# Batched cluster-routed attention and a sigmoid-gated FFN on one core: one-pass logits for late pieces, one query group turned by DMA, spare matmuls and half-step places

## The chip, the cores and the metric

The kernel runs on one core of a Trainium2 chip. The metric is device time in microseconds (us) for one execution, a median of runs. The engines are TensorE (PE; its weight loads are shown apart as PEld), VectorE (DVE), ScalarE (ACT), GpSimd (POOL) and SyncE (SP), which here only issues DMAs. Each engine works off its own instructions in the order in which they were written, and waits on semaphores for the others.

## The reference

Inputs are q, k and v of 4 batches x 8 heads x 768 rows x 64 columns, 16 centroids for each head, and three FFN matrices. Each query row and each key row is given to the centroid of its head with the largest dot product; a query attends only to the keys of its own cluster. The output of attention is the input of a gated FFN.

```python
q_assign = np.argmax(np.einsum('bhsd,hcd->bhsc', q_n, c_n), axis=-1)
k_assign = np.argmax(np.einsum('bhsd,hcd->bhsc', k_n, c_n), axis=-1)
mask = q_assign[:, :, :, None] == k_assign[:, :, None, :]
scores = scale * np.matmul(q, k.transpose(0, 1, 3, 2))
scores = np.where(mask, scores, -1000000000.0)
...
gate = 1.0 / (1.0 + np.exp(-(x @ w_gate)))
val = x @ w_val
return (gate * val @ w_out).astype(np.float32)
```

x has 3072 rows and 512 columns, the FFN is 1536 wide. All inputs are float32; the kernel multiplies in float16.

## The kernel before

**Operands.** For each head a tile T holds 12 blocks of 128 columns: blocks 0 to 5 are the keys, 6 to 11 the queries, transposed, so that rows 0 to 63 are the high half of each value in float16. At first rows 64 to 127 hold the low half (the rest of the value), which makes the logits exact enough; after the clusters are picked, rows 64 to 79 are overwritten by a one-hot row of the cluster (keys) or by -1920 times the cluster's complement (queries). One score matmul then gives the masked scores.

**Pieces.** The way of one head from rows to T goes in pieces, whose names stand in the table SCHED: hi (cast to float16; 0 for keys, 1 for queries), lo (subtraction for the low half), tu (transposes on TensorE into PSUM), ev (evacuation to T), lg (logits: T against the centroids), pk (maximum and comparison), ot (the one-hot rows transposed), pl (placed into rows 64 to 79 of T). h1 to h7 are heads 1 to 7 of batch 0, with all keys and the first three query blocks; r0 to r3 are the last three query blocks of pairs 0 to 3 of batch 0, both heads of a pair together; g0 and g1 are heads 0 and 1 of batch 1. The other heads of batches 1 to 3 (names b1p1..., b2...) are transposed by DMA (tn), their one-hot rows too, and copied into T by small DMAs (hp). Pieces of batch 0 and g0, g1 have logits in two passes (`logits2`, L320: for each block one matmul with the high half of the centroids and one with the low half, 16 columns each, added up in PSUM). The others have them in one pass (`logits`, L332: one matmul of 32 columns for each block, a copy of the low half by ScalarE or VectorE, L341, and an addition by VectorE, L349). `b{b}p{p}l2{e}` chooses two passes for one head, if true; `b{b}p{p}le{e}` puts the copy on VectorE, if true.

**Steps.** The attention is a list of steps; a step is one key block against three query blocks of one head: a score matmul (`sc`, L541), an exponential on ScalarE (`es`, L546) and, three steps later (two after batch 0), three matmuls with the values (`av`, L558). Batch 0 has 96 steps: all heads with the first three query blocks (steps 0 to 47), then all with the last three (48 to 95). Each later batch has 96 as well. After the score matmul of a step come, in this order, gate and value matmuls or output matmuls of the FFN, as far as a credit allows (`ns...`, by 24 steps), the `av` matmuls of an earlier step, and the background work that SCHED places at that step (`run_bg`). SCHED thus fixes by hand, for every engine's queue, where each piece stands; places are whole steps. `nd<i>` puts that many spare matmuls of 128 columns, whose result is overwritten, ahead of the score matmul of step i; `dm0` to `dm4` do so in the lead-in and at step 0.

**Turning x.** The result of a pair (`xp`, L299, by GpSimd) is transposed to xTb, the FFN's input, either on TensorE (L577, evacuated at L578) or by a DMA transpose from SyncE (L580). `xm{p}0` chooses TensorE for the first half of a pair of batch 0, `xt...` is a delay in steps. For the second half the code of before looks up `xm{p}1`, which is not in the table, so that TensorE is taken for pair 3 alone.

**FFN.** A block of 384 rows takes 24 groups of four matmuls for gate (L397) and value (L412), with tanh on ScalarE (L403) and a product on VectorE (`hT`, L417), then nine groups of four output matmuls (L429). The weights come by DMAs from GpSimd's queue (`w00` to `w31`, L198, and `wo0`, `wo1`, L204), which stand in GpSimd's order among its computing. The first block starts at step 57.

**Buffers.** Score, gate, value and logits tiles share a ring of four PSUM banks (`bank`), transposes of pieces and output tiles share two (`turns`, the pool `op`). The raw rows of a pair lie in four buffers a side, so that the loads of batch 1 wait in SyncE's queue until batch 0 has used them.

Of the kernel before, what the change touches and what calls it, by code (L numbers as in the profile page):

```python
# [8 lines left out]
FP = mybir.dt.float32  # L9
# [6 lines left out]
SCHED = {  # L16
# [58 lines left out]
def kernel(  # L75
# [23 lines left out]
    TINY = 1e-30  # L99

# [17 lines left out]
    esp = pool("es", 6)  # L118
# [51 lines left out]
    def load_chunks(eng, side, p, part):  # L170
        if part == 0:
            RAW[side, 0, p] = raw(side)
        c = slice(3 * part, 3 * part + 3)
        eng.dma_start(out=RAW[side, 0, p][:, :, c], in_=view(side, 0, p)[:, :, c])

    def load_half(eng, side, part):
        if part == 0:
            RAW[side, 0, 0] = raw(side)
        c = slice(3 * part, 3 * part + 3)
        eng.dma_start(out=RAW[side, 0, 0][:, 0, c], in_=view(side, 0, 0)[:, 0, c])  # L180
# [6 lines left out]
    load_head(SP, "q", 0, 1, slice(0, 3))  # L187
# [8 lines left out]
    def load_w(i, j):  # L196
        for t, src in (((wg[i], moe_w_gate), (wv[i], moe_w_val))[j],):
            POOL.dma_start(  # L198
                out=t.rearrange("p dc fc f -> p dc (fc f)"),
                in_=src.rearrange("(dc p) (g f) -> p dc g f", p=128, f=WQ * 128)[:, :, i, :],  # L200
            )

    def load_wo(i):
        POOL.dma_start(  # L204
            out=wo[i],
            in_=moe_w_out.rearrange("(g fc p) m -> p g fc m", g=2, p=128)[:, i],
        )
# [38 lines left out]
    def v_cast(b, p, cast=None):  # L246
        va = VA[b, p] = vas[(b * NP + p) % len(vas)]
# [84 lines left out]
    def logits(t, h, n, copy=None):  # L332
        lg = bank(512, name="lg")
        for c in range(n):
            PE.matmul(  # L335
                out=lg[:, bass.ts(c, 32)], lhsT=t[:, c, :],
# [6 lines left out]

    def pick(lg, parts):

        if isinstance(lg, tuple):
            ls = smp.tile([128, 12, NCL], FP, name="lgs")
            n = lg[0].shape[1]
            DVE.tensor_tensor(ls[:, 0:n], lg[0], lg[1], ALU.add)  # L349
            lg = ls[:, 0:n]  # L350
# [37 lines left out]
    def ffn_atoms(xT, t0, n, b, ch, final=False):  # L388
# [4 lines left out]
        def gate(fc, st):  # L393
            def f():
                g = bank(512, name="g")
# [12 lines left out]
        def val(fc, st):  # L408
            def f():
                w = bank(512, name="v")  # L410
# [12 lines left out]
        def outp(t, part, st):  # L423
            def f():
                if part == 0:
                    st.append(op.tile([128, DM], FP, tag="o", name="o"))
# [92 lines left out]
    def head_steps(b, p, e, halves):  # L519
        t = T[b, 2 * p + e]  # L520
        steps = []
        order = [(j, i) for j in range(NCH) for i in range(len(halves))]
        for j, i in order:
            for c in halves[i : i + 1]:
                steps.append(dict(
                    b=b, p=p, e=e, nq=3 * len(halves), k=t[:, j, :], h0=halves[0],
                    q=t[:, 6 + 3 * c : 9 + 3 * c, :], j=j, c0=3 * i,
# [6 lines left out]

    def do_scores(s):
        sc = bank(384, name="sc")
# [8 lines left out]
        es = esp.tile([128, 384], HP, name="es")  # L545
# [522 lines left out]
```

## Time and profile before

| | |
|---|---|
| median of 3 runs | 337.14 us (336.45 to 338.35) |
| the profiled execution | 337.21 us |
| its span, first to last instruction | 335.1 us |
| instructions in the profile | 9001 |
| score matmuls / FFN gate, value / output matmuls | 384 / 384, 384 / 276 recorded and 36 at the end |
| two-pass logits matmuls / one-pass | 240 / 264 |
| spare matmuls in steps | 39 |
| step 0, step 57, step 75 (start of the score matmul) | 8.28, 45.55, 60.81 us |

The span lies inside the execution; 2.1 us are around it. Durations of single matmuls in the profile are longer than their pace, since one starts before the last has drained: for prices the distance between starts is used. Idle times are given with the instruction that seems to have ended them.

### The profile page before, as it was taken

The page shows a single profiled execution, that of the slowest core. Times are in us where ns is not written, and L with a number is a line of the kernel's source. Part 1 is how long each engine was busy: PE and PEld are TensorE (multiplying, and loading weights), DVE is VectorE, ACT ScalarE, POOL GpSimd, SP SyncE. Part 2 cuts the span into 40 slices and gives each one's busy share as a digit, 9 for nine tenths or more (in the row PEclk, how much of TensorE's full clock was granted, in tenths as well). Part 3 has the DMA queues.
Part 4 walks back from the last instruction along what each step waited for, and adds up shares of the span by engine and source line. Part 5 has one row for each costly group of instructions (what it writes and reads, how often), then busy time and mean ns, then how long its engine had stood idle before and what let it go on. Part 6 is the DMA issues. An engine that isn't in the chain of part 4 may idle for free.

```text
span 335.1 us, 9001 instructions
## 1 busy us (share of the span) xinstructions
PE 325.0 (97%) x3422; PEld 210.5 (63%) x3422; DVE 186.2 (56%) x530; ACT 235.8 (70%) x543; POOL 109.8 (33%) x151
## 2 busy tenths in 40 slices
PE   7798999999999999999999999999999999999996
PEld 4587866766666666666556665666556655654654
DVE  6668756786667777465547654466434331340431
ACT  6488987766998888877768876787677876532321
POOL 6668455442154444413242343323201010100000
PEclk9699999999999999999999999999999999999999
DMA  7999999744986989596457754952612022101002
GB/s 211 354 156 135 204 212 194 101 145 104 243 222 114 230 206 197 151 185 198 94 179 171 180 102 112 254 96 49 132 71 47 14 25 74 46 0 64 32 0 96
DMA packets 80523, 45.25 MB, mean 135 GB/s; under 512 B 57376, under 2 KB 77536, under 8 KB 80480
## 3 DMA queue, kind: packets, MB, share of 16 engines
q1 hardware_dynamic: 74400, 39.83, 49.8%
q0 software_dynamic: 5792, 4.72, 10.2%
q8 instruction: 27, 0.44, 0.6%
q10 hardware_dynamic: 288, 0.13, 0.2%
q14 instruction: 16, 0.13, 0.1%
HBM read 28.34 MB, written 6.29 MB: 103 GB/s over the span
## 4 chain that ended last, share of the span: by engine, by line
PE 86%; DMA 6%; DVE 2%; POOL 2%; SPq 2%; issue 1%; ACT 0%; POOLq 0%; DVEq 0%; ACTq 0%
PE o L429 18%; PE v L412 17%; PE g L397 17%; PE sc L541 16%; PE av L558 9%; DMA T<-hl 4%; PE lg L335 2%; DMA qraw<-in_q_dram 2%; PE lg L326 1%; PE t_ps L720 1%; POOL hl L708 1%; PE o_end L453 1%; SPq L163 1%; POOL wv L198 1%; DVE T L731 1%
## 5 line engine op out<-in xcount | busy, mean ns | idle before, releaser
L546 ACT ACTIVATE es<-sc 128x384 f16<-128x384 f32 x384 | 173.2, 493 | 41.6 <-PE sc L541 25.5
L541 PE MATMUL sc<-T 128*128 128x384 f16 x384 | 117.2, 327 | 0.7 <-DVE T L775 0.2
L558 PEld LDWEIGHTS <-es 128*128 128x128 f16 x1152 | 82.1, 98 | 44.8 <-issue 0.8
L558 PE MATMUL av<-va,es 128*128 128x65 f16 x1152 | 97.7, 194 | 0.0
L417 DVE SCALAR_TENSOR_TENSOR hT<-th,v 128x384 f16<-128x384 f32 x96 | 53.2, 554 | 71.5 <-PE av L558 45.7
L397 PE MATMUL g<-xTb,wg 128*128 128x384 f16 x384 | 78.0, 326 | 0.2
L412 PE MATMUL v<-xTb,wv 128*128 128x384 f16 x384 | 78.0, 326 | 0.0
L429 PE MATMUL o<-wo,hT 128*128 128x512 f16 x276 | 68.7, 379 | 0.0
L299 POOL TENSOR_TENSOR xp<-t,rec 128x192 f16<-128x192 f32 (+1 forms) x46 | 29.3, 637 | 115.2 <-DVE rec L296 75.2
L403 ACT ACTIVATE th<-g 128x384 f32<-128x384 f32 x96 | 47.2, 492 | 25.2 <-DVE hT L417 16.2
L397 PEld LDWEIGHTS <-wg 128*128 128x128 f16 x384 | 37.3, 97 | 21.3 <-issue 1.2
L412 PEld LDWEIGHTS <-wv 128*128 128x128 f16 x384 | 37.4, 97 | 20.6 <-issue 0.7
L429 PEld LDWEIGHTS <-hT 128*128 128x128 f16 x276 | 26.9, 98 | 23.1
L541 PEld LDWEIGHTS <-T 128*128 128x128 f16 x384 | 37.3, 97 | 0.8 <-DVE T L775 0.6
L957 POOL TENSOR_TENSOR hl<-kraw,hl 128x384 f16<-128x384 f32 x22 | 20.5, 930 | 34.1 <-DVE hl L956 18.1
L294 DVE TENSOR_TENSOR t<-av,sv 128x195 f32<-128x195 f32 (+1 forms) x46 | 20.1, 437 | 20.5 <-PE av L558 19.2
L957 POOL TENSOR_TENSOR hl<-qraw,hl 128x384 f16<-128x384 f32 x22 | 20.1, 912 | 20.2 <-DVE hl L956 20.2
L438 ACT ACTIVATE ob<-o 128x512 f32<-128x512 f32 x15 | 9.0, 597 | 12.3 <-PE o L429 12.0
L349 DVE TENSOR_TENSOR lgs<-lg,lglo 128x192 f32<-128x192 f32 x22 | 7.8, 357 | 14.8 <-ACT lglo L341 14.4
L436 DVE TENSOR_SCALAR ob<-o 128x512 f32<-128x512 f32 x8 | 5.5, 691 | 16.8 <-PE o L429 16.8
L248 POOL CAST va<-vraw 128x768 f16<-128x768 f32 x16 | 13.9, 872 | 0.4 <-DMA vraw<-in_v_dram 0.4
L335 PE MATMUL lg<-cm,T 128*128 128x32 f16 x264 | 10.0, 176 | 0.7 <-DMA T<-hl 0.7
(112 smaller groups left out, 246.2 us busy)
## 6 DMA issues: line engine op xcount, KB each, us to landing
vraw<-in_v_dram SPq DMA_DIRECT2D x16, 384.0 KB, 5.0
out_dram<-ob SPq DMA_DIRECT2D x23, 256.0 KB, 2.2
kraw<-in_k_dram SPq DMA_DIRECT2D x15, 384.0 KB, 3.9
qraw<-in_q_dram SPq DMA_DIRECT2D x12, 384.0 KB, 4.2
wg<-in_moe_w_gate_dram POOLq DMA_DIRECT2D x4, 384.0 KB, 5.9
wv<-in_moe_w_val_dram POOLq DMA_DIRECT2D x4, 384.0 KB, 6.0
wo<-in_moe_w_out_dram POOLq DMA_DIRECT2D x2, 768.0 KB, 10.3
qraw<-in_q_dram SPq DMA_DIRECT2D x7, 192.0 KB, 7.3
```

The costliest lines, as they stand in the source:

```text
L294: DVE.tensor_tensor(t[:, 0:nq, :], av, sv, ALU.add)
L299: (eng or POOL).tensor_tensor(x, t[:, 0:nq, 0:64], bcast(rec[:, 0:nq], 64), ALU.mult)
L335: PE.matmul(out=lg[:, bass.ts(c, 32)], lhsT=t[:, c, :], rhs=cm[:, h].rearrange("p s n -> p (s n)"), start=True, stop=True,)
L397: PE.matmul(out=g[:, 0:n], lhsT=wg[fc // WQ][:, dc, fc % WQ, :], rhs=xT[:, dc, t0 : t0 + n], start=(dc == 0), stop=(dc == NDC - 1),)
L403: ACT.activation(th[:, 0:n], g[:, 0:n], AF.Tanh, scale=0.5)
L412: PE.matmul(out=w[:, 0:n], lhsT=wv[fc // WQ][:, dc, fc % WQ, :], rhs=xT[:, dc, t0 : t0 + n], start=(dc == 0), stop=(dc == NDC - 1),)
L417: DVE.scalar_tensor_tensor(hT[:, fc, 0:n], st[0][:, 0:n], 1.0, w[:, 0:n], ALU.add, ALU.mult)
L429: PE.matmul(out=o, lhsT=hT[:, fc, bass.ts(t, 128)], rhs=wo[fc // 6][:, fc % 6, :], start=(fc == 0), stop=(fc == NFC - 1),)
L541: PE.matmul(out=sc.rearrange("p (c t) -> p c t", t=128), lhsT=s["k"], rhs=s["q"], start=True, stop=True,)
L546: ACT.activation(es, sc, AF.Exp, scale=SCALE)
L558: PE.matmul(out=av[:, s["c0"] + i, :], lhsT=s["es"][:, bass.ts(i, 128)], rhs=VA[b, p][:, e, s["j"], :], start=(first and i == 0), stop=(la ...
L957: POOL.tensor_tensor(hl[:, :, 64:128], r, hl[:, :, 0:64], ALU.subtract)
```

## The change

1. Pieces may have logits in one pass: a flag for g0 and g1 (`gL` = 1), one for each of r0 to r3 (`rL2`, `rL3` = 1, the others 0). Copy and addition then stand in the piece lg.
2. The rows of r3 (`rD3` = 1) are transposed by two DMAs, one for each head, in place of six transposes on TensorE and two evacuations. A like flag for g0 and g1 is 0.
3. `nd...`: 39 spare matmuls become 29, placed anew; one is left from step 48 on, ahead of step 57. `dm4` is 3 and was 0.
4. Places may be half steps: a piece at x.5 stands right after the next step's score matmul, ahead of its FFN and `av` matmuls. Most places of batch 0 and of g0 and g1 change by half a step to four, some of batch 1 too.
5. Pieces change engines (a name with E: A is ScalarE, D VectorE, P GpSimd), x of pair 0's first half goes from TensorE to DMA (`xm00` = 0), `xm13`, `xm23`, `xm03` are 0, so that those DMA transposes are not delayed any more, and the lookup for the second halves is now `xm{p}3`.
6. The code can cut the query blocks otherwise than three and three (`q0`, not in the table, so 3), and asserts that each piece follows what it needs.

```diff
     def logits(t, h, n, copy=None):
+        return logits1([(t, c, h) for c in range(n)], copy)
+
+    def logits1(groups, copy=None):
+        n = len(groups)
         lg = bank(512, name="lg")
-        for c in range(n):
+        for i, (t, c, h) in enumerate(groups):
             PE.matmul(
-                out=lg[:, bass.ts(c, 32)], lhsT=t[:, c, :],
+                out=lg[:, bass.ts(i, 32)], lhsT=t[:, c, :],
                 rhs=cm[:, h].rearrange("p s n -> p (s n)"), start=True, stop=True,
             )
...
+    def join(a, c):
+        n = a.shape[1]
+        ls = smp.tile([128, 12, NCL], FP, name="lgs")
+        DVE.tensor_tensor(ls[:, 0:n], a, c, ALU.add)
+        return ls[:, 0:n]
...
-        if b == 0 and SCHED.get(f"xm{p}{o // 384}", p == 3):
+        if b == 0 and SCHED.get(f"xm{p}{3 if o else 0}", p == 3):
...
     def run_bg(i):
-        for f in bg.pop(i, []):
-            f()
+        for x in sorted(x for x in bg if x <= i):
+            for f in bg.pop(x):
+                f()
...
         def lg(part=0):
+            if SCHED.get("gL", 0):
+                st["lg", part] = join(*logits(T[b, h], h, 12))
+                return
...
         def tu(eng=None):
-            st["ps"] = bank(768, HP, name="t_ps") if SCHED.get("rb", 0) else turns(name="t_ps")
+            if SCHED.get(f"rD{p}", 0):
+                for e in range(2):
+                    SP.dma_start_transpose(
+                        out=T[0, 2 * p + e][:, 6 + Q0 : 12, :],
+                        in_=st["hl"][:, e].rearrange("p c x -> p (c x)"),
+                    )
+                return
...
         def ev(e, eng=None):
+            if SCHED.get(f"rD{p}", 0):
+                return
...
+            st["lg"] = join(*logits1(gs)) if SCHED.get(f"rL{p}", 0) else logits2(gs)
...
                 do_scores(s)
+                run_bg(step_no[0] - 0.5)
                 pend.append(s)
```

Of the table, the entries that the text comes back to (before, then after):

```
vs00 4, 0.5       w00 3, 0          w10 10, 7         w11 10, 10
h1lo1E -, D       h2hi1E -, A       h3lo1E -, D       h6lo1E -, D
h5hi0E P, -       h5hi0 10, 10.5    h5lo0 11, 11.0    h5tu0 17, 16.5
h6hi0 22, 19.5    h6lo0 23, 22.0    h6tu0 25, 25      h6tu1 26, 25
h5ot 26, 27.5     h5pl0 27, 28.0    h5pl1 27, 27.5
r3lo 66, 65.0     r3loE -, D        r3tu 70, 68.5     r3lg 75, 74.5
r2lg 65, 64.0     g0tu0 75, 74      g0lg 81, 81.5     g1lg 91, 91.5
xm00 1, 0         ql2 16, 14        b1p2l20 0, -0.5   dm4 0, 3
b1p1le0 0, 0.5    b1p1le1 0, -3     b1p2le1 0, 3.5    lag10 8, 7.5
ns2 490, 510      ns3 500, 460      ns12 280, 290     wo0 56, 55.5
```

Spare matmuls before: steps 8, 11 (3), 14 (2), 16, 18 (2), 23, 26, 30 (2), 31 (3), 34 (2), 36, 41 (2), 44 (2), 46 (3), 59, 65 (3), 67, 68 (2), 73, 78, 82 (3), 98. After: 7, 8, 14 (2), 16 (3), 21, 22 (3), 26, 31 (3), 32, 34 (2), 35 (3), 36, 39 (2), 41 (2), 44 (2), 57.

More of the change, by code (lines that the diff above doesn't have):

```diff
@@ L99 @@
     TINY = 1e-30
+    Q0 = SCHED.get("q0", 3)
+    NB = 128 * max(Q0, NCH - Q0)
+    PARTS = {0: (0, Q0), 1: (Q0, NCH - Q0)}
     ctx.enter_context(tc.manual_schedule())
@@ L172, in load_chunks @@
             RAW[side, 0, p] = raw(side)
-        c = slice(3 * part, 3 * part + 3)
+        c = slice(PARTS[part][0], sum(PARTS[part]))
         eng.dma_start(out=RAW[side, 0, p][:, :, c], in_=view(side, 0, p)[:, :, c])
@@ L178, in load_half @@
             RAW[side, 0, 0] = raw(side)
-        c = slice(3 * part, 3 * part + 3)
+        c = slice(3 * part, 3 * part + (3 if side == "k" else Q0))
         eng.dma_start(out=RAW[side, 0, 0][:, 0, c], in_=view(side, 0, 0)[:, 0, c])
@@ L186 @@
     load_head(SP, "k", 0, 1)
-    load_head(SP, "q", 0, 1, slice(0, 3))
+    load_head(SP, "q", 0, 1, slice(0, Q0))
     WQ = 3
@@ L342, in logits @@
         return lv[:, :, 0, :], lo[:, 0:n]
+    def join(a, c):
[3 more added lines that the diff above has]
+        return ls[:, 0:n]
     def pick(lg, parts):
         if isinstance(lg, tuple):
[L347 to L350, printed above, removed]
+            lg = join(*lg)
         n = lg.shape[1]
@@ L394, in f @@
             def f():
+                need(("w", fc // WQ, 0), *(("x", b, p, t0 // 128 + c) for p in range(NP) for c in range(n // 128)))
                 g = bank(512, name="g")
@@ L521, in head_steps @@
         steps = []
-        order = [(j, i) for j in range(NCH) for i in range(len(halves))]
-        for j, i in order:
-            for c in halves[i : i + 1]:
+        cuts = [PARTS[c] if b == 0 else (3 * c, 3) for c in halves]
+        for j in range(NCH):
+            for c, (a, n) in zip(halves, cuts):
                 steps.append(dict(
-                    b=b, p=p, e=e, nq=3 * len(halves), k=t[:, j, :], h0=halves[0],
-                    q=t[:, 6 + 3 * c : 9 + 3 * c, :], j=j, c0=3 * i,
+                    b=b, p=p, e=e, nq=sum(z for _, z in cuts), k=t[:, j, :], h0=cuts[0][0],
+                    h1=c, q=t[:, 6 + a : 6 + a + n, :], j=j, c0=a - cuts[0][0], n=n,
                 ))
@@ L533, with ready @@
     cur = {}
+    def ready(s):
+        b, h = s["b"], 2 * s["p"] + s["e"]
+        if (b == 0 or (b, s["p"]) in PEP) and b + h:
+            need(f"{'hg'[b]}{h}pl0", f"{'hg'[b]}{h}pl1")
+            if b == 0 and s["h1"]:
+                need(f"r{s['p']}pl{s['e']}")
+        if b == 0 and h == 0 and s["h1"]:
+            need("r0pl0")
+        if b and (b, s["p"]) not in PEP:
+            need((b, s["p"], "hp0"), (b, s["p"], "hp1"))
     def do_scores(s):
-        sc = bank(384, name="sc")
+        ready(s)
+        sc = bank(128 * s["n"], name="sc")
         for _ in range(SCHED.get(f"nd{step_no[0]}", 0)):
@@ L556, in do_av @@
         av, x = cur["av"], cur["x"]
-        for i in range(3):
+        for i in range(s["n"]):
             PE.matmul(
@@ L560, in do_av @@
                 rhs=VA[b, p][:, e, s["j"], :],
-                start=(first and i == 0), stop=(last and i == 2), skip_group_check=True,
+                start=(first and i == 0), stop=(last and i == s["n"] - 1), skip_group_check=True,
             )
@@ L572, in turn_x @@
     def turn_x(b, p, x, o, nq, xT):
+        done.update(("x", b, p, o // 128 + c) for c in range(nq))
         dst = xT[:, p, o : o + 128 * nq].rearrange("p (c t) -> p c t", t=128)
-        if b == 0 and SCHED.get(f"xm{p}{o // 384}", p == 3):
+        if b == 0 and SCHED.get(f"xm{p}{3 if o else 0}", p == 3):
             ps = (turns if SCHED.get("lgop", 1) else bank)(NCH * 128, HP, name="x_ps")
@@ L585, in at @@
     def at(i, f):
-        bg.setdefault(max(i, step_no[0]), []).append(f)
+        bg.setdefault(max(i, step_no[0] - 0.5), []).append(f)
     def plan(name, step, f):
@@ L591, in run_bg, with need @@
     def run_bg(i):
-        for f in bg.pop(i, []):
-            f()
+        for x in sorted(x for x in bg if x <= i):
+            for f in bg.pop(x):
+                f()
+    done = set()
+    def need(*names):
+        for n in names:
+            assert n in done, n
     LA = {0: SCHED.get("la0", 3), 1: SCHED.get("la1", 2)}
@@ L694, in rng @@
             n = NCH // parts
-            return (6, 9) if s else (n * part, n * part + n)
+            return (6, 6 + Q0) if s else (n * part, n * part + n)
         def hi(s, eng=None, part=0):
@@ L808, in lg @@
         def lg(eng=None):
-            st["lg"] = logits2(
-                [(T[0, 2 * p + e], 9 + c, 2 * p + e) for e in range(2) for c in range(3)]
-            )
+            gs = [(T[0, 2 * p + e], 6 + Q0 + c, 2 * p + e) for e in range(2) for c in range(N)]
+            st["lg"] = join(*logits1(gs)) if SCHED.get(f"rL{p}", 0) else logits2(gs)
         def pk(eng=None):
@@ L815, in pk @@
             mx = smp.tile([128, 18], FP, name="mx")
-            DVE.tensor_reduce(mx[:, 0:6], st["lg"], AX.X, ALU.max)
+            DVE.tensor_reduce(mx[:, 0 : 2 * N], st["lg"], AX.X, ALU.max)
             DVE.tensor_tensor(
-                oh_view(st["oh"], 1, 2, 2, 3),
+                oh_view(st["oh"], 1, 2, 2, N),
                 st["lg"].rearrange("p (h c) n -> p h c n", h=2),
-                bcast(mx[:, 0:6].rearrange("p (h c) -> p h c", h=2), NCL), ALU.is_lt,
+                bcast(mx[:, 0 : 2 * N].rearrange("p (h c) -> p h c", h=2), NCL), ALU.is_lt,
             )
         def ot(eng=None):
-            st["ot"] = (
-                bank(384, HP, name="oh_ps") if SCHED.get("rb", 0) else turns(384, name="oh_ps")
-            )
-            for c in range(3):
+            st["ot"] = turns(128 * N, name="oh_ps")
+            for c in range(N):
                 PE.transpose(st["ot"][:, bass.ts(c, 128)], st["oh"][:, c, :], identh)
@@ L915, in put, with go @@
         g = lambda *x: f(*x) if key not in ("tu", "lg", "pk", "ot", "hp") else f(*x[:-1])
-        plan(nm, u + off, lambda: g(*arg, eng))
+        pre = nm[: len(nm) - len(key) - len(arg)]
+        tail = "".join(str(a) for a in arg)
+        before = {
+            "hi": ["ql" + nm[1]] if nm[0] == "r" else [], "lo": ["hi" + tail],
+            "tu": ["hi" + tail, "lo" + tail], "ev": ["tu"] if nm[0] == "r" else ["tu" + tail],
+            "lg": ["ev0", "ev1"], "pk": ["lg"], "ot": ["pk"], "pl": ["ot"],
+        }[key]
+        before = [x if x[:2] == "ql" else pre + x for x in before]
+        def go():
+            need(*before)
+            g(*arg, eng)
+            done.add(nm)
+        plan(nm, u + off, go)
     FIRST = dict(hi0=-18, lo0=-18, hi1=-17, lo1=-17, tu0=-13, ev0=-12, tu1=-12, ev1=-11,
@@ L981, in go, with g @@
             o = SCHED.get(f"b{b}p{p}{name}" if b < 2 else f"b2{name}", off)
-            at(use + o, f)
+            def g():
+                if name[:2] == "tn":
+                    need((b, p, f"sp{name[2]}0"), (b, p, f"sp{name[2]}1"))
+                if name == "ot":
+                    need((b, p, "pk0"), (b, p, "pk1"))
+                f()
+                done.add((b, p, name))
+            at(use + o, g)
         for e in range(0 if (b, p) in PEP else 2):
@@ L1017 @@
                 break
-            at(u + lag, lambda xT=xT, b=b, i=i: ffn_block(xT, 384 * i, 384, b, CH[i]))
+            c0, cn = PARTS[i] if b == 0 else (3 * i, 3)
+            for w in range(1 + (cn > 3)):
+                z = cn // (1 + (cn > 3))
+                at(u + lag, lambda xT=xT, b=b, a=c0 + z * w, n=z: ffn_block(
+                    xT, 128 * a, 128 * n, b, list(range(a, a + n))))
         for p, e, c in heads(b):
```

47 lines of the change are left out of this document (32 added, 15 removed), and 113 rows, old and new, of the table SCHED.

## The prediction

> **What bounds the kernel now.** I read the page first: busy shares, clock slices, chain.
>
> ```profile
> PE 325.0 (97%) x3422; PEld 210.5 (63%) x3422; DVE 186.2 (56%) x530; ACT 235.8 (70%) x543; POOL 109.8 (33%) x151
> PEclk9699999999999999999999999999999999999999
> PE 86%; DMA 6%; DVE 2%; POOL 2%; SPq 2%; issue 1%; ACT 0%; POOLq 0%; DVEq 0%; ACTq 0%
> ```
>
> TensorE is busy 97% of the span and is 86% of the chain that ended last; its clock is below full in one slice only. So the kernel is bound by TensorE, but an average does not say where an idle moment is still left. The windows do (us, then busy time of PE, PEld, DVE, ACT and POOL with instruction counts, granted clock, DMA share, GB/s):
>
> ```profile
> 8.00:16.00 8.00, 5.56 (x75) 4.19 (x74) 4.83 (x15) 3.06 (x7) 5.36 (x9) 0.70 1.06 354
> 16.00:24.00 8.00, 8.00 (x138) 6.96 (x136) 5.66 (x20) 7.23 (x18) 5.37 (x8) 0.87 1.09 184
> ```
> ```profile
> 18.00:36.00 18.00, 16.70 (x313) 14.07 (x311) 13.99 (x46) 15.09 (x35) 14.76 (x22) 1.00 0.97 126
> 36.00:46.00 10.00, 9.71 (x156) 7.32 (x154) 7.76 (x27) 9.50 (x24) 3.82 (x7) 1.00 1.26 255
> 46.00:335.00 289.00, 284.97 (x2814) 179.56 (x2811) 154.05 (x416) 201.41 (x464) 80.15 (x101) 1.00 0.54 122
> ```
>
> From 46 us on (the first gate matmul, step 57; a step is one score matmul, counted in the timeline from step 0 at 8.28 us), TensorE idles 4.0 us of 289: there only matmuls that go away, or new waits, count. Up to 36 us it idles and runs slowly. From 36 to 46 us ScalarE (9.50 of 10, one exponential every 0.375 us) is as full as TensorE, so a matmul more or less is worth little.
>
> The price of a small matmul is its pace, start to start, not its duration. From the timeline of TensorE:
>
> ```profile
> 88.67 0.45 PE L335 MATMUL lg<-cm,T 128*128 128x32 f16 x12
> 88.97 0.32 PE L541 MATMUL sc<-T 128*128 128x384 f16 x1
> ```
> ```profile
> 85.46 0.33 PE L577 MATMUL x_ps<-identh,xp 128*128 128x128 f16 x3
> 85.62 0.33 PE L541 MATMUL sc<-T 128*128 128x384 f16 x1
> ```
>
> Twelve logits matmuls take 88.97 - 88.67 = 0.30 us, 25 ns each (16 columns pace the same: the row at 23.75 in the same view has six in 0.15). A 128-column transpose or spare matmul takes 0.16/3 = 55 ns.
>
> **The change, part by part.** *TensorE's own work.* One-pass logits for g0 and g1 (24 to 12 each) and for r2 and r3 (12 to 6 each) remove 36; but b1p2l20 becomes -0.5, which counts as true, so head 4 of batch 1 goes to two passes and adds 12: net -24 x 25 ns = -0.60. r3 by DMA: -6 x 55 ns = -0.33. x of pair 0 by DMA (xm00 1 to 0): -3 x 55 = -0.17. Spare matmuls in steps: 39 to 29 = -0.55 (from step 57 on 13 go; nd57, just ahead of step 57, stays). dm4: +3 = +0.17. Sum **-1.48 us**; of it -1.65 lies after 46 us, on the bound engine, where nothing hides or eats it.
>
> *What the one-pass form adds.* For each of the four pieces a ScalarE copy (317 ns for 128x192) and a VectorE addition (357 ns), which now stands inside the logits step and so queues on VectorE before the evacuations of v (hT). After 46 us VectorE is busy 154 of 289 and ScalarE 201 of 289, which hides the work. Not hidden is VectorE standing for ScalarE: in the waits, "DVE lgs L349 <- ACT lglo L341" is 14.4 us in 12 times, 1.2 each. Four of these are between 0 (four PSUM buffers of the ring cover them, as they do for the twelve, with all TensorE idling at 4.0 us) and 4.8. Nearest is the covered case: **+0.3**. Three logits copies of batch 1 go from ScalarE to VectorE (354 ns each), hidden likewise.
>
> *The start.* Steps 0 to 5 take 9.9 us (8.28 to 18.18). TensorE, then VectorE:
>
> ```profile
> 8.93 0.50 PE L720 MATMUL t_ps<-identh,hl 128*128 128x128 f16 x6
> 11.07 0.40 PE L720 MATMUL t_ps<-identh,hl 128*128 128x128 f16 x3 [1.64 <-POOL hl L708]
> ```
> ```profile
> 9.45 0.35 DVE L701 CAST hl<-qraw 128x192 f16<-128x192 f32 x1 [0.75 <-DMA qraw<-in_q_dram]
> 9.72 0.91 DVE L701 CAST hl<-kraw 128x384 f16<-128x384 f32 x1
> 10.66 0.35 DVE L771 COPY T<-oh_ps 16x384 f16<-16x384 f16 x1
> ```
>
> The trace names GpSimd as releaser of the 1.64 us, but the third transposing group needs one of two PSUM buffers, and L771, which frees it, ends at 11.01, stuck behind a cast that waits 0.75 for q of pair 1. The change gives that cast to ScalarE (h2hi1E) and puts h1's subtraction there instead (no load to wait for, 0.36 to 0.62 by VectorE's rows of that kind). L771 then ends near 10.0, and 0.6 to 1.0 us is saved; the three dm4 matmuls and pair 0's six v sums (vs00, 4 to 0.5) fall into idle time. I take -0.6, since half of the saving is run at the reduced clock.
>
> *Steps 6 to 36.* The two largest waits are for GpSimd: 0.43 us at 24.56 (h5, whose subtraction stands behind two weight issues of 0.80 and 0.75 at 22.02 and 22.82) and 0.83 at 30.33 (h6, whose cast on VectorE came at step 22). GpSimd, then TensorE:
>
> ```profile
> 27.85 0.80 POOL L198 DMA_DIRECT2D wg<-in_moe_w_gate_dram  x1
> 28.67 0.72 POOL L299 TENSOR_TENSOR xp<-t,rec 128x192 f16<-128x192 f32 x1
> 29.37 0.90 POOL L708 TENSOR_TENSOR hl<-kraw,hl 128x384 f16<-128x384 f32 x1
> ```
> ```profile
> 30.33 0.51 PE L720 MATMUL t_ps<-identh,hl 128*128 128x128 f16 x6 [0.67 <-POOL hl L708]
> ```
>
> The change starts w00 at 0 and w10 at 7, so weight issues leave the way of h5; casts h6 at 19.5 with the subtraction at 22 and gives its query half to VectorE. Both waits go (1.26), with some of the 0.70 of smaller ones that follow them at steps 20 and 22. Late next: h5's placing, two steps ahead of its first use with 0.92 us of VectorE work (copies of 0.36 and 0.56) in some 1.1 us, and the doubled transposes at step 25. TensorE idles 1.3 us in 18 to 36 by the view and some 2.5 by pace; I take -1.1, bounds +1.5 (as many new waits) and -2.5. The early part is **-1.7**.
>
> *r3 by DMA.* Two transposes enter SyncE's queue between xTb of pair 0's second half and T of batch 1's head 2. The latter is pushed by 2 x 1.2 us of issue; it landed at 62.0 and is used at step 82 (68.4), so nothing is late. r3's own logits stand on TensorE at step 75, in order, ahead of gate matmuls. In the clock of before they are due at 60.81 (step 75) + 0.16 - 0.92 (removed since step 57: 8 spare matmuls, 6 transposes, 6 logits matmuls) + 0.33 (g0's transposes, moved ahead) = 60.4. r3's subtraction ends near 54.5, the issues near 55.7. But the two loads of wo (46.85 and 47.74, landing after 7.7 and 13.0) fill the DMA engines; the xTb transpose issued at 52.17 shows it, as its own query answers:
>
> ```profile
> DMA to landing us min/median/max: 8.7/8.7/8.7
> ```
>
> It landed at 60.9, the T transpose of 56.17 (5.8) at 62.0, so r3 should land at 60.0 to 61.5: a wait of 0 to 1.1. **+0.5**. At worst the second issue (55.8) also takes 8.7 and lands at 64.5: 4.1.
>
> [...]
>
> *Other moves.* xTb of pair 0 stands in SyncE's queue before r2's rows and batch 1's first loads, until GpSimd's xp (25.5); the rows are cast at 41.98, the loads used after 57 us: covered. The order of gate, value and output blocks against the steps is the same to step 155 and shifts by a step or two up to 194. At 0; bound +-0.8, a fifth of the 4.0.
>
> **Sum.** The profiled execution took 337.21 (span 335.1 and 2.1 around it); the median is 337.14, 0.07 below, so no correction. 337.21 - 1.48 + 0.3 - 1.7 + 0.5 = 334.83: **334.8**, 0.7% faster. 0.5% (335.45 to 338.83) is about what a measurement of this kernel can tell from no change.
>
> **Rivals.** *The early waits only move* (0.23): every half step trades one queue's wait for another's. For it: VectorE, ScalarE and GpSimd are all 78 to 84% busy in 18 to 36 us. Against: the two GpSimd waits have plain causes that go. 334.8 + 1.7 = 336.5.
>
> *The clock stays up* (0.13): it was at half speed for some 7 us (a mean of 0.70 over 8 us is 4.8 us at half, 0.87 is 2.1), after the idle stretch at 9.4 to 11.1 that the change shortens. That cost at most 3.4 us; ScalarE's 7.23 of 8 behind it leaves half: 334.8 - 1.7 = 333.1. [...]
>
> *r3 comes late* (0.12), the slower side: the DMA stretch of 34 to 60 us does not move with TensorE, and r3 lands at 64.5. TensorE, 1.7 earlier, then waits 5.8 at step 75: 337.21 - 1.48 + 0.3 - 1.7 + 5.8 = 340.1. It makes the kernel slower by over 0.5% from a landing at 63.3.
>
> The forecast has 0.52, of which a fifth lies within 0.5%. So faster 0.42 + 0.13 = 0.55, same 0.10 + 0.23 = 0.33, slower 0.12. The range: 332.6 (clock up, and half a us more of the early part) to 337.2 (early waits moved and a wait of 1.2 for r3); outside are the late r3 and a little below.
>
> **What would show it.** Right: the transposes of 11.07 near 10.1; no wait of over 0.3 us for GpSimd before step 36; step 57 at 43.6 to 44.6 instead of 45.55; from there to the end 0.9 us less than 289.5 (-1.65 + 0.3 + 0.5). Wrong: a gap on TensorE ahead of six logits matmuls at step 75, over 1 us; step 57 at 45 or later; or hT standing for lgs with TensorE idle.

## The result, and the profile after

The changed kernel took **333.72 us** (median of 6), the kernel before 337.33 in 6 runs beside it: a ratio of 0.99, 95% interval 0.9854 to 0.9947. A second series on another chip gave 334.49 (12 runs) beside 336.56 (30 runs), a ratio of 0.994 (0.9914 to 0.9966). One of the first six, the profiled one, ran at a mean clock of 0.656 and took 469.86 us (the median of the other five is 333.23), so the profile read here is of the second series. Its execution took 336.56 us, the longest of the twelve, with a span of 334.8; 2 us longer than the median, it may well hold more waits than a usual execution.

From its page, the same three lines as for the kernel before:

```profile
PE 322.2 (96%) x3382; PEld 207.7 (62%) x3382; DVE 188.9 (56%) x533; ACT 236.2 (71%) x546; POOL 108.6 (32%) x148
PEclk9999999999999999999999999999999999999999
PE 82%; DMA 8%; DVE 5%; ACT 3%; issue 1%; SPq 0%; POOL 0%; ACTq 0%; DVEq 0%; POOLq 0%
```

Two things differ. The clock is full in every slice, also the second, which showed 6. And DMA now has 8% of the chain that ended last, TensorE 82 in place of 86: somewhere TensorE has begun to wait for transfers. The windows, with the columns as before, say where:

```profile
8.00:16.00 8.00, 6.80 (x116) 5.34 (x114) 6.26 (x21) 5.51 (x13) 7.14 (x10) 1.00 1.07 353
18.00:36.00 18.00, 17.23 (x320) 14.27 (x318) 15.18 (x51) 15.90 (x38) 11.93 (x19) 1.00 1.24 206
46.00:335.00 289.00, 279.68 (x2727) 174.95 (x2724) 154.61 (x412) 198.36 (x457) 77.72 (x96) 1.00 0.55 120
```

Up to 16 us TensorE got 116 matmuls done in place of 75. After 46 us, where it had idled 4.0 us of 289, it idles 9.3 (289.00 - 279.68). TensorE's own timeline shows the two sides, first the start, then step 75 and step 117, with SyncE's DMA issues below them (the dots mark a gap in time):

```profile
9.06 0.50 PE L775 MATMUL t_ps<-identh,hl 128*128 128x128 f16 x6
9.80 0.33 PE L775 MATMUL t_ps<-identh,hl 128*128 128x128 f16 x3 [0.24 <-DVE T L826]
```
```profile
56.24 0.24 PE L350 MATMUL lg<-cm,T 128*128 128x32 f16 x3
58.16 0.24 PE L350 MATMUL lg<-cm,T 128*128 128x32 f16 x3 [1.68 <-DMA T<-hl]
```
```profile
91.02 0.26 PE L592 MATMUL av<-va,es 128*128 128x65 f16 x3
92.70 0.46 PE L350 MATMUL lg<-cm,T 128*128 128x32 f16 x12 [1.43 <-DMA T<-hl]
```
```profile
47.60 1.19 SPq L615 DMA_TRANSPOSE xTb<-xp  x1
50.05 2.51 SPq L851 DMA_TRANSPOSE T<-hl  x2
...
81.59 0.42 SPq L171 DMA_DIRECT2D kraw<-in_k_dram  x1
82.07 0.50 SPq L171 DMA_DIRECT2D qraw<-in_q_dram  x1
82.61 0.47 SPq L171 DMA_DIRECT2D vraw<-in_v_dram  x1
83.19 2.50 SPq L401 DMA_DIRECT2D T<-ohT  x4
85.85 0.47 SPq L460 DMA_DIRECT2D out_dram<-ob  x1
86.41 2.13 SPq L330 DMA_TRANSPOSE T<-hl  x1
```

The group that waited 1.64 us for GpSimd at 11.07 now starts at 9.80 after 0.24. Step 75's first three logits matmuls (r3's first head) run, the other three wait 1.68 for the second transpose, issued at 51.3, landed at 58.1. At step 117 twelve logits matmuls of batch 1 wait 1.43 for a T transpose that stands in SyncE's queue behind the next pair's loads: issued at 86.41, landed at 92.7, 6.2 us. In the kernel before it stood behind them too, went out at 89.60 and landed at 94.2, 4.6 us later and 0.1 ahead of its use; the one for step 153, issued at 108.69, landed at 115.9 and held TensorE up for 0.34:

```profile
89.60 2.44 SPq L319 DMA_TRANSPOSE T<-hl  x1
94.28 0.39 PE L335 MATMUL lg<-cm,T 128*128 128x32 f16 x9
115.92 0.47 PE L335 MATMUL lg<-cm,T 128*128 128x32 f16 x12 [0.34 <-DMA T<-hl]
```

So TensorE came 3.2 us earlier to step 117 (90.86 in place of 94.03), and the transpose was issued 3.2 earlier as well, but it landed only 1.5 earlier, since it took 1.6 longer to land. All of TensorE's waits for T transposes, before and then after (us in all, times, longest):

```profile
PE lg L335 <- DMA T<-hl: 0.7, 2, 0.3
PE lg L350 <- DMA T<-hl: 4.7, 4, 1.7
```

### The profile page after: what moved, and what is told of

It is laid out like the page before. It is cut to its first block, busy times and chain, and to the rows that moved or that the text cites. A ratio compares the mean times of both kernels' runs of the same rounds, so it can differ in the third digit from the quotient of the medians.

```text
span 468.1 us, 8923 instructions
## 1 busy us (share of the span) xinstructions
PE 462.1 (99%) x3382; PEld 261.2 (56%) x3382; DVE 188.7 (40%) x533; ACT 242.6 (52%) x546; POOL 107.8 (23%) x148
## 4 chain that ended last, share of the span: by engine, by line
PE 95%; DVE 2%; DMA 1%; SPq 0%; issue 0%; ACT 0%; DVEq 0%
PE v L432 20%; PE g L416 20%; PE o L450 19%; PE sc L574 19%; PE av L592 11%; PE lg L350 1%; DMA kraw<-in_k_dram 1%; PE lg L337 1%; PE o_end L474 1%; PE oh_ps L812 1%; PE t_ps L775 1%; PE sc L571 1%; PE t_ps L687 0%; DVE hl L763 0%; DVE T L786 0%; PE vs_ps L289 0%
## 5 line engine op out<-in xcount | busy, mean ns | idle before, releaser
L574 PE MATMUL sc<-T 128*128 128x384 f16 x384 | 151.8, 410 | 0.0
L592 PEld LDWEIGHTS <-es 128*128 128x128 f16 x1152 | 103.1, 117 | 78.0 <-issue 12.6
L592 PE MATMUL av<-va,es 128*128 128x65 f16 x1152 | 121.5, 223 | 0.0
L432 PE MATMUL v<-xTb,wv 128*128 128x384 f16 x384 | 112.0, 430 | 0.0
L416 PE MATMUL g<-xTb,wg 128*128 128x384 f16 x384 | 111.5, 430 | 0.0
L450 PE MATMUL o<-wo,hT 128*128 128x512 f16 x276 | 100.4, 513 | 0.0
L310 POOL TENSOR_TENSOR xp<-t,rec 128x192 f16<-128x192 f32 (+1 forms) x46 | 29.7, 645 | 189.2 <-DVE rec L307 115.9
L432 PEld LDWEIGHTS <-wv 128*128 128x128 f16 x384 | 45.2, 118 | 37.9
L416 PEld LDWEIGHTS <-wg 128*128 128x128 f16 x384 | 44.6, 117 | 37.5 <-issue 0.8
L450 PEld LDWEIGHTS <-hT 128*128 128x128 f16 x276 | 32.6, 119 | 40.2 <-issue 33.5
L362 DVE TENSOR_TENSOR lgs<-lg,lglo 128x192 f32<-128x192 f32 (+1 forms) x25 | 8.7, 349 | 27.6 <-ACT lglo L356 27.2
L350 PE MATMUL lg<-cm,T 128*128 128x32 f16 x288 | 11.7, 180 | 0.0
```

The source lines that it names most:

```text
L310: (eng or POOL).tensor_tensor(x, t[:, 0:nq, 0:64], bcast(rec[:, 0:nq], 64), ALU.mult)
L350: PE.matmul(out=lg[:, bass.ts(i, 32)], lhsT=t[:, c, :], rhs=cm[:, h].rearrange("p s n -> p (s n)"), start=True, stop=True,)
L416: PE.matmul(out=g[:, 0:n], lhsT=wg[fc // WQ][:, dc, fc % WQ, :], rhs=xT[:, dc, t0 : t0 + n], start=(dc == 0), stop=(dc == NDC - 1),)
L432: PE.matmul(out=w[:, 0:n], lhsT=wv[fc // WQ][:, dc, fc % WQ, :], rhs=xT[:, dc, t0 : t0 + n], start=(dc == 0), stop=(dc == NDC - 1),)
L450: PE.matmul(out=o, lhsT=hT[:, fc, bass.ts(t, 128)], rhs=wo[fc // 6][:, fc % 6, :], start=(fc == 0), stop=(fc == NFC - 1),)
L574: PE.matmul(out=sc.rearrange("p (c t) -> p c t", t=128), lhsT=s["k"], rhs=s["q"], start=True, stop=True,)
```

## The experiments

The theory: the start is what the change brings, and the late part's saving (spare and logits matmuls) is given back as waits for transposes by DMA, which do not land as much earlier as TensorE comes. The rivals: the late saving is real and the start small; or VectorE's added work, or the credits of the FFN, take it back.

A kernel's clock falls in some executions and not in others, and the mean granted clock of each run tells which: 0.998 or more (it never fell), 0.992 to 0.995 (3.4 us at half speed, by the profiles that show it), 0.988 to 0.990 (6.8 us). The 94 runs of before beside these experiments average 335.40 (29 that never fell), 336.45 (51) and 337.75 (14). Below, "at full clock" means the mean of the runs of the first kind; the intervals are those of all runs. Where each side has six runs or more, a difference between two such means is good to 0.4 to 0.9 us (95%, from the scatter of the runs); with fewer it can be worse.

| kernel | median (runs) | ratio to before, 95% | at full clock (runs) | before there |
|---|---|---|---|---|
| changed kernel again | 334.49 (12) | 0.994 (0.9914–0.9966) | 334.65 (11) | 335.69 (6) |
| early part alone | 335.57 (12) | 0.998 (0.9948–1.0012) | 334.53 (6) | 335.69 |
| late part alone | 337.00 (12) | 1.0019 (0.9993–1.0045) | 334.68 (1) | 335.69 |
| r3 on TensorE | 333.71 (7) | 0.9929 (0.99–0.9958) | 333.76 (6) | 335.69 |
| start undone | 335.38 (12) | 0.9991 (0.997–1.0011) | 335.31 (5) | 335.35 (12) |
| start alone | 334.18 (12) | 0.9953 (0.9935–0.9971) | 334.16 (11) | 335.35 |
| without dm4 | 335.21 (12) | 0.9982 (0.9958–1.0005) | 334.83 (9) | 335.35 |
| loads behind T | 333.05 (6) | 0.9921 (0.989–0.9951) | 332.64 (5) | 335.35 |
| start, loads behind T | 334.62 (12) | 0.9957 (0.9938–0.9976) | 334.60 (11) | 335.29 (11) |
| start, no late spare | 336.19 (12) | 0.9988 (0.9962–1.0013) | 335.11 (8) | 335.29 |
| start, late, loads behind T | 333.91 (12) | 0.9944 (0.9922–0.9965) | 333.74 (10) | 335.29 |
| late, loads behind T | 334.99 (12) | 0.9959 (0.9932–0.9986) | 334.05 (3) | 335.29 |

Three chips served, one for each four rows.

**The changed kernel again**, unaltered, for the profile above.

> The changed kernel once more, for a profile at full clock. The sum of the prediction: step 57 (first gate matmul) at 43.6 to 44.6 us in place of 45.55, the rest 0.9 us shorter than 289.5, 334.8 in all. The rival that the clock stays up: no stretch at half clock between 11 and 18 us, step 57 near 42.3, 333.1 in all. The rival that r3 comes late: a gap of over 1 us on TensorE ahead of the logits matmuls of step 75.

At full clock the change is worth 1.0 us (335.69 to 334.65); the difference of the means of all runs is 2.0, since 24 of 30 runs of before lost clock and only 1 of 12 of the changed kernel.

**The early part alone.** The changed table with two-pass logits, r3 on TensorE, and the 13 spare matmuls of step 59 on.

```diff
- gL 1   rL2 1   rL3 1   rD3 1
+ gL 0   rL2 0   rL3 0   rD3 0   nd59 1  nd65 3  nd67 1  nd68 2  nd73 1  nd78 1  nd82 3  nd98 1
```

> The new places and engines, but logits of g0, g1, r2, r3 in two passes again, r3 turned on TensorE and the 13 spare matmuls of step 59 to 98 back. By the prediction's terms the late part is worth 1.95 us of TensorE work less 0.8 of new waits: this kernel is 1.1 us slower than the changed one, with step 57 at the same time. If new waits eat the late part whole, it equals the changed kernel within 0.3 us. If the late part is all that counts, it equals the kernel before.

At full clock 334.53, as the whole change (334.65, with 0.8 either way): by these runs the late part adds nothing to the early one. Here 6 of 12 runs lost clock, which brings the median to 335.57. Step 57 starts at 41.28, but from there to the end it takes 291.5 us, 2.0 more than before, and 2.39 us are lost in one wait at step 201 for a T transpose. That wait stands although the late work was put back. This kernel keeps the change's other moves after step 57 (credits, delays, places of batches 1 and 2), so it is not shown whether it is the earlier TensorE or these moves that meet the transfer.

**The late part alone.** The table of before with

```diff
+ gL 1  rL2 1  rL3 1  rD3 1; r2lg and all r3 places as changed
- nd59 nd65 nd67 nd68 nd73 nd78 nd82 nd98   (13 spare matmuls)
```

> The table of before with one-pass logits for g0, g1, r2, r3, r3 turned by DMA with its new places, and no spare matmuls from step 57 on; everything else where it was. TensorE has 36 logits matmuls, 6 transposes and 13 spare matmuls less: 0.90 + 0.33 + 0.72 = 1.95 us. By the prediction 0.8 of it is eaten by waits: 1.1 us faster than before, step 57 as before. If r3 is late by over a microsecond, a gap ahead of its logits at step 75 shows and the gain is near nothing. If the clock follows the spare matmuls, it falls somewhere after step 57 and the kernel is slower than before.

No gain: 337.00, ratio 1.0019; in the runs with 3.4 us at half clock 336.76 (8) beside 336.52 (18) of before. In the waits view (what TensorE waited for: us in all, times, longest) the loss has a name:

```profile
PE lg L350 <- DMA T<-hl: 2.4, 3, 1.1
```

Before had 0.7 in 2 times. By steps these are 1.06 at step 75 (r3), 1.32 at 177 and 0.56 at 201 beyond TensorE's own pace (a step's time less the paces of its matmuls); the profile's time from step 57 to the end is 289.5, that of before. Of TensorE's work 1.95 us went (13 x 55 + 36 x 25 + 6 x 55 ns) and came back whole.

**r3 on TensorE.** The changed kernel with `rD3` 0.

> The changed kernel, but r3 turned by six transposes on TensorE and two evacuations at the same places. The prediction gives the DMA form -0.33 of TensorE work and +0.5 of waiting at step 75: this kernel would be the same within 0.3 us. If r3 lands in time, this one is 0.3 us slower from step 57 to the end; if r3 lands late by over 1 us, this one is faster by 0.7 or more.

333.76 at full clock (6 runs) beside 334.65 (11): by these, turning r3 by DMA costs 0.9 us, though the difference is barely clear of noise and the intervals of all runs overlap. Its six logits matmuls of step 75 now run in one group:

```profile
56.06 0.33 PE L574 MATMUL sc<-T 128*128 128x384 f16 x1
56.22 0.30 PE L350 MATMUL lg<-cm,T 128*128 128x32 f16 x6
```

The waits for T at 117, 177 and 201 stay (2.4 us in 3 times), so they are not r3's doing.

**The start undone.** The changed kernel with the pieces of h1 to h3 up to step 1, their engines, `vs00`, `vc00` and `dm4` as before.

```diff
- h1hi0 -5.5 h1lo0 -2.5 h1hi1 -4.5 h1lo1 -1.5 h2lo0 -2 h2hi1 -1.5 h3hi0 -1.5 vs00 0.5 vc00 -2.5 dm4 3 h1lo1E D h2hi1E A h3lo1E D
+ h1hi0 -4   h1lo0 -4   h1hi1 -4   h1lo1 -1   h2lo0 -1 h2hi1 -1   h3hi0 -1   vs00 4   vc00 -3   dm4 0
```

> The changed kernel with the pieces of heads 1 to 3 before step 1 (hi, lo and their engines), the first value sums and dm4 as before. If the TensorE wait at step 0 is what closed the clock gate, the clock falls to half again for 3.4 to 6.8 us near 11 us, step 6 starts 2.4 to 3.8 us later than in the changed kernel's new profile (14.4), step 57 near 44, and the waits for T after it shrink, so that the total is 0 to 2 us longer than the changed kernel. If the later places keep the clock up, step 6 is only 0.6 to 1 us later and the clock stays at full.

At full clock 335.31 beside 335.35, and 7 of 12 runs lost clock: without the start nothing that shows is left of the gain. The wait is back, and step 6 starts 1.3 us later than in the changed kernel's profile; the clock stayed up in this execution all the same (see the last section):

```profile
10.70 0.33 PE L775 MATMUL t_ps<-identh,hl 128*128 128x128 f16 x3 [1.14 <-POOL hl L763]
```

**The start alone.** The table of before with just these entries as changed.

> The table of before with these few pieces before step 1, the first value sums and dm4 as in the change, and nothing else of it. If the start is what keeps the clock up, no stretch at half clock, step 6 near 14.5, step 57 near 42 (before 45.55). Then, if waits for T by DMA eat the early gain, the rest grows from 289.5 to over 290.5 and the whole is 1.5 to 2.5 us faster than before; if nothing eats it, 3.5 us faster.

334.16 at full clock beside 335.35, and 11 of 12 runs kept the clock. These dozen entries give what the whole change gives; the 3.5 us expected if nothing eats the gain are 2.0 by medians, since that figure was reckoned from the profiled execution of before, which has the long fall of the clock. In its profile step 57 starts at 42.63 and the rest takes 289.8, 0.3 more than before: nothing of the early gain is eaten, and the only waits for T by DMA come to 0.5 us. So TensorE's coming earlier does not by itself bring waits; here the transposes came earlier with it (the one for step 117 was issued at 87.04 and landed at 91.80, 2.4 earlier than before).

**Without dm4.** The changed kernel without the three spare matmuls at step 0.

> The changed kernel without the three spare matmuls at step 0. If they keep the clock up, it falls for 3.4 to 6.8 us and step 57 comes 1.5 to 3 us later. If the shortened wait does it by itself, the profile is that of the changed kernel within 0.2 us to step 57.

3 of 12 runs lost clock, beside 2 of 17 with them: too few to tell. The profiled execution is one of the three: half speed from 11.4 to 14.8, after a wait of 0.95 for L826 where the changed kernel waited 0.24. But VectorE's cast ahead of L826 took 1.07 us in it, with a subtraction by GpSimd running all through, and 0.35 in the changed kernel's profile, with GpSimd idle; so this wait cannot be put down to dm4. At full clock 334.83, so the three matmuls cost nothing that shows. The step 75 wait is nearly gone here (0.18 beyond the pace in steps 72 to 76), as TensorE reached step 57 at 42.67 in place of 41.04.

**Loads behind T.** The changed kernel with r3 on TensorE and three T transposes ahead of the next pair's loads of k, q and v in SyncE's queue.

```diff
- rD3 1   b1p2tn1 -38   b1p3ld -69.5   b2ld -82.5
+ rD3 0   b1p2tn1 -45   b1p3ld -67     b2ld -73
```

> The changed kernel with r3 on TensorE (as in the run before), and with the T transposes of the later pairs ahead of the loads of k, q and v of the next pair in SyncE's queue (b1p2tn1 -38 to -45, b1p3ld -69.5 to -67, b2ld -82.5 to -73). If the waits of the logits matmuls at steps 117, 177 and 201 (1.0, 1.05 and 0.85 us in the profile with r3 on TensorE) come from these loads standing ahead, they go and the kernel is 2 to 2.9 us faster than that run's 333.7. If the transposes are late for themselves, or the loads become late, it is not faster.

333.05, at full clock 332.64 (5): 2.7 less than before, and 1.1 less than with r3 on TensorE alone, or 0.8 when each is held against its own before (other chips, with befores of 335.35 and 335.69). The waits went as expected, but of the 2 to 2.9 us expected for them at most half came. It is the lowest median of the series, but its interval overlaps those of the changed kernel and of r3 on TensorE, so that it beats before is shown, that it beats the changed kernel is likely and no more. SyncE's queue, and TensorE's waits for T:

```profile
80.56 1.49 SPq L330 DMA_TRANSPOSE T<-hl  x1
82.10 0.86 SPq L171 DMA_DIRECT2D kraw<-in_k_dram  x1
83.02 0.49 SPq L171 DMA_DIRECT2D qraw<-in_q_dram  x1
83.55 0.47 SPq L171 DMA_DIRECT2D vraw<-in_v_dram  x1
```
```profile
PE lg L350 <- DMA T<-hl: 0.4, 1, 0.4
```

The transpose for step 117 goes out at 80.56 in place of 86.41 and lands at 84.3, 3.7 us later, 6 us before its use. Of the 2.4 us of such waits with r3 on TensorE, and the 4.7 in the changed kernel's profile, 0.4 are left. From step 57 to the end this profile takes 289.4 where that with r3 on TensorE takes 290.9.

**Start, with loads behind T.** Start alone and the three entries above (`b1p3ld` is -67 in the table of before already).

> The table of before with the pieces of heads 1 to 3 up to step 1 as changed (start alone, which ran at 334.2) and, besides, the three transposes of T of batch 1's pairs 2 and 3 and of batch 2's first pair set ahead of the next pair's k, q and v loads in SyncE's queue. In the profile of start alone TensorE waited for T by DMA once, 0.5 us, and lost 0.45 at step 89 and 0.70 at step 187. Theory (the loads ahead of T matter only once TensorE has less to do): nothing to gain but that 0.5, so 333.5 to 334.3. Rival (the order of these transfers is worth the same 1 us or more whatever TensorE does): 333.2 or less.

334.60 at full clock beside 334.16 of start alone (other chips): no gain, 0.3 above the range given for it, and the rival's 333.2 is out. The order of the queue by itself is worth nothing; it was not late for the pace of before. The wait for T at step 187 is 1.1 us here, 0.5 in start alone.

**Start, without the late spare matmuls.** Start alone less 13 spare matmuls.

> The table of before with the changed start alone and without the 13 spare matmuls of step 59 and later: 13 x 55 ns = 0.72 us of TensorE work less, nothing else moved. Theory (after 46 us the transposes of T by DMA set the pace, and TensorE only waits longer for them): no gain over the 334.2 of start alone, 333.9 to 334.5, with new waits of logits for T at steps 117, 177 or 201 of some 0.7 in all. Rival (it is the work that counts, as the prediction had it): 333.5, with no such waits.

336.19, and 335.11 at full clock (8): 0.72 us of TensorE's work taken out and nothing gained; beside start alone (334.16, another chip) 0.95 lost, with 0.7 either way. That it gains nothing is as the theory had it; the time is above its 333.9 to 334.5, and a loss is in neither forecast. The wait of step 153, from TensorE's timeline:

```profile
111.77 0.25 PE L592 MATMUL av<-va,es 128*128 128x65 f16 x3
113.16 0.47 PE L350 MATMUL lg<-cm,T 128*128 128x32 f16 x12 [1.14 <-DMA T<-hl]
```

That transpose was issued at 105.82, right after three loads, and landed at 113.1. In start alone it landed at 112.6 and TensorE came to its use only at 112.9: so spare matmuls stood where a wait would have been.

**Start and late part, loads behind T.** Start alone, less the 13 spare matmuls, one-pass logits for g0, g1, r2 and r3, r3 on TensorE, T ahead of the loads: 1.62 us of TensorE's work less.

> The table of before with the changed start alone, without the 13 late spare matmuls, with one-pass logits for g0, g1, r2 and r3 (36 matmuls of 25 ns less), r3 turned on TensorE, and T ahead of the loads as above: 0.72 + 0.90 = 1.62 us of TensorE work less after 46 us. Theory (that work counts once the transposes of T come in time): 1.0 to 1.6 less than start alone, 332.6 to 333.2. Rival (something else, VectorE or ScalarE in the logits steps or the credits of the FFN, takes it back anyway): 333.8 or more.

The median of 333.91 misses the theory's range and lies in the rival's. At full clock 333.74 is 0.86 less than start with loads behind T on the same chip (good to 0.3), about half of the 1.62, and 0.4 less than start alone on another. Something still takes the other half. TensorE's waits in the profile have no new one of over 0.2 us for VectorE or ScalarE; the largest new one is for another transfer, the FFN's input, at step 192 (the credits of the FFN were not varied):

```profile
133.57 0.65 PE L416 MATMUL g<-xTb,wg 128*128 128x384 f16 x3
135.13 0.32 PE L416 MATMUL g<-xTb,wg 128*128 128x384 f16 x1 [0.91 <-DMA xTb<-xp]
```

**The late part, loads behind T, with the start of before.**

> The table of before, start included, without the 13 late spare matmuls, with one-pass logits for g0, g1, r2 and r3, r3 turned on TensorE, and T ahead of the loads. Late alone, which had the loads ahead of T and r3 by DMA, ran at 337.0 beside 336.6 of before. Theory (transfers took the gain): 1.0 to 1.6 less than before in runs of the same clock, so 334.8 to 335.4 at the median. Rival (the gain is lost elsewhere): 336.0 or more.

334.99, inside the theory's range. In runs with 3.4 us at half clock 335.10 (8) beside 336.43 (17) of before, at full clock 334.05 (3) beside 335.29: 1.2 to 1.3 less. The late part alone, which differs in the queue's order and in r3's way (by DMA, which cost 1.06 us at step 75), gave +0.2 in the same comparison. So most of the work taken off TensorE counts once the transfers come in time, and in late alone and start without late spare, where they did not, none of it does. How much of the difference is the queue's and how much r3's these two runs do not tell.

## Why the prediction was right, and where it was not

334.8 was forecast in a range of 332.6 to 337.2; 333.72 and 334.49 were measured. The time is right, but in part by luck. The start, put at -0.6, was worth 1.7 to 2.0 with its clock (start alone, by means and by medians of all runs). Steps 6 to 36, at -1.1, and the late part, at -1.48 + 0.3 + 0.5 = -0.7, were worth nothing that shows in the time. These errors cancel.

*What bounds the kernel: failed in part.* "There only matmuls that go away, or new waits, count" holds, but I read an idle time of 4.0 us in 289 as slack in the other engines. The transposes for steps 117 and 153 landed at 94.2 and 115.9 and were used at 94.28 and 115.92: already level with TensorE. An engine that is 97% busy can have a second chain right beside it. Start without late spare shows it best.

*TensorE's own work, -1.48: the size was right (40 matmuls fewer, as reckoned), its effect was not.* Late alone took it out and gained nothing (1.0019); late with loads behind T gained 1.2 to 1.3 of it.

*One-pass logits, +0.3: nothing speaks against it.* The changed kernel's waits have 0.3 us in all of gate matmuls waiting for hT, once; a stall of hT for lgs with TensorE idle does not show. No run has the one-pass form as its only difference.

*The start, -0.6: cause right, size too small.* The third transposing group starts at 9.80, L826 ends at 9.74 (near 10.0 forecast). Undoing the start takes the whole gain away and the start alone gives it, 1.2 us at full clock. With it the rival **the clock stays up** came true (chance 0.13, 333.1): with the new start, dm4 included, 18 of 90 runs lost clock (five of the first series among them), with the old one 92 of 130. The fall costs 1.05 us (3.4 us long) or 2.35 (6.8 us). The window of the fall in the kernel before:

```profile
8.28:11.20 2.92, 1.14 (x13) 0.78 (x13) 2.07 (x6) 0.90 (x2) 2.27 (x5) 1.00 1.04 350
11.20:18.00 6.80, 6.36 (x80) 5.21 (x79) 3.15 (x11) 3.72 (x7) 3.67 (x5) 0.50 1.10 343
```

After 2.92 us in which TensorE was busy 1.14, 6.80 us at half speed. The profiled execution of before was thus of the most costly kind, 337.21, and 0.9 above the mean of 336.3 of its 94 runs: its agreement with a median of three hid that, and "no correction" was a step that failed.

*Steps 6 to 36, -1.1: wrong in size.* The GpSimd waits went, as said (none above 0.3 before step 36; the 0.43 and 0.83 of the prediction are by pace, its rows show 0.67 for the second), but the stretch took 18.46 us in place of 18.63, -0.2. By losses beyond TensorE's pace steps 18 to 36 fell from 2.0 to 1.5, and steps 6 to 12 rose from 0.13 to 0.63: with TensorE at full speed from the start, the pieces that follow are late, which fits start alone, where steps 6 to 12 lose 0.97. Against start alone, which takes 19.3 there, the new places do save 0.9. As early alone is no faster than start alone at full clock (334.53, 334.16), the saving buys no time by itself. Steps 36 to 57, where the prediction gave nothing, took 8.19 us in place of 8.74.

*Step 57 at 43.6 to 44.6: it was 41.04*, by the start and the clock: steps 0 to 6 took 5.99 us, not 9.90.

*r3 by DMA, +0.5: mechanism right, size wrong.* Steps 72 to 76 lost 2.2 us in the profile, and r3 on TensorE saves 0.9 by runs. The transposes took 6.1 and 6.8 us to land, between the bounds of 5.8 and 8.7; the landing, 58.1, was at the forecast's early end (60.0 less the 1.7 of the early part is 58.3). What was off was TensorE: 56.4 at step 75, where 60.4 less 1.7 was reckoned. At that 58.7 nothing would have waited. The prediction put the slow landing down to the loads of wo. The first of these transposes landed 0.4 after the second wo load (55.8); but in the same profile T transposes issued at 86.41 and 121.59, long after wo, took 6.2 and 7.1 us. So wo's share is not shown.

*The rest, 0.9 less than 289.5: wrong.* It took 293.7 in this profile, the longest execution of the twelve: 4.2 more. 4.0 of that is the waits for T (4.7 for 0.7), none of which the prediction had but r3's.

*Other moves, 0 within 0.8: wrong for SyncE's queue.* The order of T transposes and loads was looked at for r3 and batch 1's head 2 only, not for steps 117 to 201. Three entries of the table there are worth some 0.8 to 1.1 us with r3 on TensorE, and nothing at the pace of before.

Open stays why early alone lost its clock in 6 of 12 runs with the new start (its profile is of a run at full clock and shows no fall), what start without late spare lost its 0.95 us to, and which further transfers would have to move for all 1.6 us of the late part to count beside the start.

## What to carry to other kernels

Before work is taken off the bound engine, compare for each transfer the landing with its use: where they are level, spare work on that engine cost nothing here (0.72 us of it taken out of start alone: 335.11 at full clock in place of 334.16), and late work taken out brought nothing (1.0019) until the transfers were moved ahead in their queue (then 1.2 to 1.3 us, with r3 on TensorE). And look at the clock of the profiled execution before it is made the base of a sum: in the one used here, the clock was at half speed for 6.8 us behind the wait of 1.6 us at the start, which by the means of the runs cost another 2.35 us, and 29 of 94 executions of the same kernel paid nothing of it. A kernel whose executions differ so in mean clock (0.988 to 1.0 here) is best compared among runs of one mean clock.

## What the runs showed of the hardware

**The clock.** Of the 94 runs of before 29 never fell, 51 lost about 1.05 us and 14 about 2.35. In the four profiles that show a fall at the start it begins at 11.2 to 11.7 us and lasts 3.4 or 6.8, after a wait of 0.95 (without dm4), 1.46 (late alone), 1.64 (before) or 2.0 us (late with loads behind T); after a wait of 1.14 (start undone) there was none. The length of the wait thus does not decide, and what does in a single execution no run here shows.

**DMA transposes.** In the profile of before, 11 of the T transposes after 70 us were issued with no load of v from SyncE's queue still in flight and landed after 3.8 us (median; 3.6 to 4.7), and 7 with 3 to 5 us of such a load still to go, and landed after 5.5 (4.4 to 7.2). In this profile and those of the twelve runs above together these are 160, after 3.8 (3.6 to 5.6), and 44, after 5.8 (4.3 to 8.1). So moving transposes ahead of the loads, as in loads behind T, brought the one for step 117 forward twice: it was issued earlier (80.56 in place of 86.41) and took less time to land (3.7 in place of 6.2).
